# Another instruction order for TensorE, from a planner with other durations, in an attention and gate kernel

## The chip, the core and the metric

The kernel runs on one core of one Trainium2 chip. The metric is the device time of one execution in microseconds. A second figure is the span of the profiled execution, from its first instruction to its last; every time inside the kernel is counted from the start of that span.

## The reference

```python
xn = _layernorm(x, axis=-1)                       # x: 2048 x 640
s = _A_ref(xn, A_wqkv, A_wo)                      # 32 heads of 20
g = _silu(_B_ref(xn, B_w1, B_w2))                 # 640 -> 1536 -> 640
return x + s * g

# _A_ref
scores = jnp.einsum("bhqd,bhkd->bhqk", q, k) * scale
p = _softmax(scores, axis=-1)
o = jnp.einsum("bhqk,bhkd->bhqd", p, v)
# _B_ref
h = jnp.maximum(jnp.einsum("bsd,df->bsf", x, w1), 0)
return jnp.einsum("bsf,fd->bsd", h, w2)
```

x is float32, and so are all weights.

## The kernel before

**Tiling.** The 2048 rows are 16 tiles of 128 rows, taken together as 4 chunks of 512. The 32 heads are 8 groups g of 4 heads, and the 4 heads of a group are two packs of two heads, one on the upper and one on the lower half of the rows of TensorE's array. Products with weights take float32 as two float16 parts, high and low, and add three products (high by high, high by low, low by high).

**Start.** Each tile of x gets its statistics on VectorE (`stats`, L362), a chunk of four tiles its factors (`normal`, L371), and then each tile is scaled on ScalarE, VectorE or POOL (L394, L397). `turn` (L408) transposes a chunk on TensorE (L417); ScalarE writes the high part (the cast of L419), and the low part (xt_lo) is made either by one VectorE operation (L517) or by a ScalarE copy and a POOL subtraction (the "rest" of L522, then L524). Meanwhile the weights of q, k and v get their peaks (`peak_of`, L1075; L229), from which a power of two is made for scaling, with two small products (L244, L256). `piece` (L432) loads 128 columns of a weight and splits them into the two parts: "fast" by ScalarE and VectorE (L280, L282: qh, kh, ql, kl), or else by three POOL operations (L284 to L288). `begin` (L1091) issues this in an order of its own. `first_qk` (L488) makes the first 128 columns of q or k of a chunk (L499); `store` and `load_pack` send them to DRAM and back as packs.

**Middle.** For each group g and chunk c of query rows there are 64 units of scores with their row maxima (L628 on TensorE, a maximum on VectorE, L632). When the 64 are there, the maxima are turned (`rows`, L657; L660) and sent into two more rows of the packed q (the eight transfers of L672, qp<-mhl). Then 64 units of transposed scores follow, from which the maxima are subtracted by those rows (L715 on TensorE, the exponential on ScalarE, L719). Four exponentials are a step; a step is weighed with v by four matmuls in float32 (`weigh`, L743; L751, "pv"). A chunk has 16 steps, the kernel 512, numbered in the names of the tiles pt0 to pt511. After the 16 steps the result is copied out of the accumulator (L763 or L766), turned (L773) and normalised. Between these stands fill: v's products (L329, later L315), the other columns of q and k, the hidden layer of the gate, its output, and the output projection (`out_first`, L998; `out_rest`, L1034), nearly all in the helper `products` (L315), on one half of the array's rows at a time.

**What sets the order.** A planner (`Plan`, L81) runs while the program is written. It holds a clock of its own for TensorE and one for each other engine, the transfers and SyncE; each operation that is written adds its assumed cost (`plan.op`, `plan.pe`, `plan.arrival`). VectorE's small work waits in a list of jobs and is taken by rank, lowest first (`job`, L109). The loop at L1230 looks at what the clocks say is ready: pairs of units (L628, L715) if the engine behind them has less than FULL of work queued, weighing, urgent small turns, the start's generators (`first`), fill (`fill`, rationed by `pace`, L1223). It also lets maxima run at most a set number of units ahead (`mx_start`, L606). The constants at L52 to L78 are the costs: EXP and RED for the exponential and the maximum, BACK for the time until a result is known elsewhere, SWITCH for a change between TensorE's modes. The chip sees only the order: each engine works its list in order and waits on semaphores where data or a buffer is missing.

The lines that the change touches are those constants, the rank of `stats` (L360), the costs at L477 to L480, L595, L874, L958, L960 and L993, and the two pieces at L1110.

Of the kernel before, what the change touches and what calls it, by code (L numbers as in the profile page):

```python
# [17 lines left out]
P = 128  # L18
# [10 lines left out]
TPC = CW // P  # L29
# [21 lines left out]

SWITCH = 100  # L52
LAG = 210
BACK = 90
PAIR = 220
PV = 850
MM = 216
MM_HALF = 136
TURN = 110
EXP = 605  # L60
RED = 640
DMA = 1900
ISSUE = 400
RAGGED = 650
# [93 lines left out]
def attention_gate(ctx: ExitStack, tc: tile.TileContext, x, wqkv, wo, w1, w2, out):  # L158
    nc = tc.nc
    ctx.enter_context(tc.manual_schedule())  # L160
    plan = Plan()
# [194 lines left out]
    def load_x(t, queue="sp"):  # L356
        xs[t] = early.tile([P, D], F32, name=f"x{t}", tag="x", bufs=XS)
        (nc.sync if queue == "sp" else nc.scalar).dma_start(xs[t], x[t * P:(t + 1) * P, :])
        x_landed[t] = plan.arrival(4 * P * D, queue=queue)
        plan.job(30 + 10 * (t // TPC) if t >= TPC else 0, x_landed[t], lambda: stats(t))  # L360

    def stats(t):  # L362
        st = lnp.tile([P, 2, 6], F32, name=f"st{t}", tag="st", bufs=TPC)
# [100 lines left out]
    def qk(m, c):  # L464

        cs = slice(c * CW, (c + 1) * CW)
        sc = SQ / (SX * SW)
        yield from when(lambda: ("q", m) in pieces and ("k", m) in pieces and c in turned)
        ws, at = zip(*(pieces[name, m] for name in "qk"))
        bs, free = take_two()  # L470
        got = yield from products([banks[b] for b in bs], [terms(w, xt, KD, slice(0, P), cs) for w in ws],
                                  max(free, xt_ready[c], *at))
        for name, b in zip("qk", bs):
            hi = stage.tile([P, CW], F16, name=f"hi{name}{m}{c}", tag="hi")
            lo = stage.tile([P, CW], F16, name=f"lo{name}{m}{c}", tag="lo")
            nc.scalar.mul(hi, banks[b], sc)
            done = plan.op("act", 520, got)  # L477
            r = stage.tile([P, CW], F32, name=f"r{name}{m}{c}", tag="r", bufs=2)
            nc.scalar.mul(r, banks[b], sc)  # L479
            bank_free[b] = done = plan.op("act", 520, got)  # L480
            nc.gpsimd.tensor_sub(lo, r, hi)  # L481
            done = plan.op("pool", 1160, done)

            plan.at(done, lambda name=name, hi=hi, lo=lo: store(name, m, c, hi, lo))
# [100 lines left out]
    def v_tiles(n, t):  # L585

        yield from when(lambda: ("v", n) in pieces and t // TPC in turned)
        w, ready = pieces["v", n]
        bs, free = take_two()
        got = yield from products([banks[b][:, 0:HD] for b in bs],  # L590
                                  [terms(xt, w, KD, slice(u * P, (u + 1) * P), slice(0, HD)) for u in (t, t + 1)],
                                  max(free, ready, xt_ready[t // TPC]))
        for u, b in zip((t, t + 1), bs):
            nc.scalar.mul(va[n][:, u, :, 0:DH], banks[b][:, 0:HD].rearrange("p (h d) -> p h d", d=DH), v_scale[n])
            bank_free[b] = v_ready[n, u] = plan.op("act", 450, got)  # L595

# [226 lines left out]
    def gate_hidden():  # L825
# [34 lines left out]
        for f in range(KF):  # L860
            fs = slice(f * P, (f + 1) * P)
            yield from when(lambda: ("1", f) in pieces)
            w, ready = pieces["1", f]
            for pr in range(NC // 2):
                two = [slice(c * CW, (c + 1) * CW) for c in (2 * pr, 2 * pr + 1)]
                bs, free = take_two()
                got = yield from products([banks[b] for b in bs], [terms(w, xt, KD, slice(0, P), cs) for cs in two],
                                          max(free, ready))
                for c, cs, b in zip((2 * pr, 2 * pr + 1), two, bs):
                    r = stage.tile([P, CW], F32, name=f"hr{c}{f}", tag="r", bufs=2)  # L870
                    hi = stage.tile([P, CW], F16, name=f"hh{c}{f}", tag="hi")
                    lo = stage.tile([P, CW], F16, name=f"hl{c}{f}", tag="lo")
                    nc.scalar.activation(r, banks[b], AF.Relu, scale=SH / (SX * SW))  # L873
                    bank_free[b] = done = plan.op("act", 520, got)  # L874
                    nc.gpsimd.tensor_copy(hi, r)  # L875
                    plan.op("pool", 610, done)
                    nc.gpsimd.tensor_sub(lo, r, hi)
                    done = plan.op("pool", 1160)

                    def store(fs=fs, cs=cs, f=f, c=c, hi=hi, lo=lo):  # L880
                        nc.sync.dma_start(h_d["h"][fs, cs], hi)
                        nc.sync.dma_start(h_d["l"][fs, cs], lo)
                        h_stored[f, c] = plan.arrival(2 * 2 * P * CW, 2)

                    plan.at(done, store)
                if pr == 0 and f + 2 < KF:
                    piece("1", w1, f + 2, P)
# [8 lines left out]
    def gate_out():  # L896
# [46 lines left out]
        for c in range(S // HW):  # L943
            ht, ready = nxt
            if c + 1 < S // HW:
                nxt = load_h(c + 1)
            for u in range(HW // P):
                t = c * (HW // P) + u
                gt = gp.tile([P, D], F32, name=f"g{t}", tag="g")
                bs, free = take_two()  # L950
                got = yield from products([banks[b][:, 0:HD] for b in bs],
                                          [terms(ht, w2t, KF, slice(u * P, (u + 1) * P), ns) for ns in halves],
                                          max(free, ready))
                for n, (b, ns) in enumerate(zip(bs, halves)):
                    ps = banks[b][:, 0:HD]
                    th = gp.tile([P, HD], F32, name=f"th{t}{n}", tag="th")
                    nc.scalar.activation(th, ps, AF.Tanh, scale=cz)
                    done = plan.op("act", 540, got)  # L958
                    nc.vector.scalar_tensor_tensor(gt[:, ns], th, 1.0, ps, op0=ALU.add, op1=ALU.mult)
                    bank_free[b] = done = plan.op("dve", 550, done)  # L960

                def store(t=t, gt=gt):
                    nc.sync.dma_start(g_d[t * P:(t + 1) * P, :], gt)
                    g_stored[t] = plan.arrival(4 * P * D)

                plan.at(done, store)
# [13 lines left out]
    def transposed(name, src, ks, ready, tag):  # L980
# [9 lines left out]
            nc.tensor.transpose(pt[:, k, :], src[:, k, :], ident)  # L990
            got = plan.pe("F", TURN, free)
        nc.scalar.mul(oh, pt, SH)
        done = plan.op("act", 520, got)  # L993
        nc.vector.scalar_tensor_tensor(ol, pt, SH, oh, op0=ALU.mult, op1=ALU.subtract)
        bank_free[b] = done = plan.op("dve", 690, done)
        return (oh, ol), done
# [71 lines left out]
    def wide(name):  # L1068
        return wqkv[:, col[name] * D:(col[name] + 1) * D]
# [21 lines left out]
    def begin():  # L1091
# [5 lines left out]
        def next_raw(k):  # L1097
            held.append(raw_load("k", k))
            if k + 1 == KD:
# [7 lines left out]
                    for j in range(2):  # L1107
                        nc.sync.dma_start(kp[i][64 * j + 3 * DH:64 * j + 3 * DH + 2, :], ones_d)
                plan.arrival(9 * 8192, 9)
                for name in "qk":  # L1110
                    piece(name, wide(name), 1, P)

        peak_of("q", 10, [raw_load("q", k) for k in range(KD)], next_raw)
        v_half(0)
# [7 lines left out]
    def settle():  # L1122
# [2 lines left out]
        early_stack.close()  # L1125
        pools["pp"] = pool(ctx, "pp", PTS)
        pools["ep"] = pool(ctx, "ep", 2)
        peaks("1", w1_rows, KF, rawp, 3000, 60000, "wr")
        packs_of(1)
        yield 0  # L1130
# [174 lines left out]
```

## Time and profile before

| | us |
|---|---|
| three runs | 1824.48, 1827.29, 1829.36 |
| median | 1827.29 |
| the profiled execution's own time | 1827.41 |
| its span | 1825.6 |
| TensorE busy | 1756.1 |
| VectorE busy | 1464.2 |
| ScalarE busy | 1397.2 |
| POOL busy | 316.7 |

The engines are PE (TensorE's matmuls), PEld (its weight loads), DVE (VectorE), ACT (ScalarE), POOL and SP (SyncE, which issues nearly all transfers). A row of the timeline gives the start, the length, the engine, the line, the operation, what is written from what, and the count; in brackets stands how long the engine stood idle ahead of it and what released it. Matmuls overlap, so the length of a row is longer than its share of the time: the distance to the next row's start is what counts. Instructions of one kind that follow each other are merged to one row.

### The profile page before, as it was taken

The numbers are of one execution on the slowest core, as the hardware profiler recorded it, in microseconds if no ns is written. First come the engines' busy times: TensorE is split into PE (matmuls) and PEld (weight loads), VectorE is DVE, ScalarE is ACT, GpSimd is POOL, SyncE is SP. The second block draws the span as 40 slices with busy tenths as digits, with TensorE's granted clock in tenths as the row PEclk, the third lists the DMA queues.
The fourth block names the chain that finished last, engine by engine and source line by source line (L and its number), as shares of the span: only waits on it lengthen the run. The fifth ranks groups of instructions, "written<-read, shape, count | busy, mean of one in ns | idle before, by whom it ended". The sixth has DMA issues, their size and how long they took to land.

```text
span 1825.6 us, 37300 instructions
## 1 busy us (share of the span) xinstructions
PE 1756.1 (96%) x14911; PEld 713.9 (39%) x14911; DVE 1464.2 (80%) x2521; ACT 1397.2 (77%) x2328; POOL 316.7 (17%) x339
## 2 busy tenths in 40 slices
PE   5999999999999999999999989999999999999988
PEld 3443334443332433333334234444444443434322
DVE  7598888888887787878887868888888888888961
ACT  2638888788887877888888857877888788786666
POOL 2612200011103454422221130000000000112210
PEclk9999999999999999999999989999999999999999
DMA  7213310201125232311112441211113003224021
GB/s 250 81 58 116 106 48 22 48 20 40 57 64 156 86 106 87 109 35 41 37 35 71 148 112 54 73 33 54 54 47 98 13 19 126 80 80 146 30 71 50
DMA packets 133750, 135.07 MB, mean 74 GB/s; under 512 B 26888, under 2 KB 110232, under 8 KB 133576
## 3 DMA queue, kind: packets, MB, share of 16 engines
q1 hardware_dynamic: 133000, 131.38, 23.6%
q8 instruction: 117, 1.92, 0.4%
q10 hardware_dynamic: 576, 1.31, 0.2%
q14 instruction: 57, 0.47, 0.1%
HBM read 85.07 MB, written 47.33 MB: 73 GB/s over the span
## 4 chain that ended last, share of the span: by engine, by line
PE 87%; ACT 5%; DVE 4%; DMA 3%; issue 1%; POOL 0%; SPq 0%; DVEq 0%; ACTq 0%
PE pv L751 27%; PE ps L315 25%; PE ps L715 15%; PE ps L628 13%; ACT pt L719 4%; PE ps L329 3%; DVE m L632 2%; PE ps L499 2%; DMA hl<-hl_d 1%; PE ps L773 1%; PE ps L990 1%; PE ps L417 0%; DMA 2p<-in_B_w 0%; DMA x<-in_A_x 0%; DMA op<-in_A_wo 0%
## 5 line engine op out<-in xcount | busy, mean ns | idle before, releaser
L632 DVE TENSOR_REDUCE m<-ps 128x1 f32<-128x512 f32 x2048 | 1283.4, 684 | 265.8 <-PE ps L628 259.6
L719 ACT ACTIVATE pt<-ps,cexp 128x512 f32<-128x512 f32 x2048 | 1256.8, 694 | 294.0 <-PE ps L715 204.3
L628 PE MATMUL ps<-kp,qp 60*128 60x512 f16 x2048 | 597.1, 380 | 13.2 <-ACT rest L522 3.9
L715 PE MATMUL ps<-qp,kp 62*128 62x512 f16 x2048 | 588.8, 380 | 5.0 <-ACT pt L719 1.8
L751 PE MATMUL pv<-pt,va 128*21 128x512 f32 x4096 | 542.1, 602 | 0.0
L715 PEld LDWEIGHTS <-kp 62*128 62x128 f16 x2048 | 148.4, 94 | 351.7 <-issue 305.0
L628 PEld LDWEIGHTS <-qp 60*128 60x128 f16 x2048 | 148.2, 94 | 129.0 <-issue 95.3
L751 PEld LDWEIGHTS pv<-pt,va 128*21 128x21 f32 x4096 | 89.6, 99 | 243.7 <-issue 223.3
L315 PE MATMUL ps<-w2th,hl 64*128 64x320 f16 x768 | 123.9, 296 | 2.9 <-DMA hl<-hl_d 2.9
L1027 POOL TENSOR_TENSOR pre<-pre,go 128x320 f32<-128x320 f32 x32 | 26.9, 863 | 572.7 <-DVE go L1025 572.7
L315 PE MATMUL ps<-w2th,hh 64*128 64x320 f16 x768 | 125.8, 296 | 0.3 <-ACT pt L719 0.3
L315 PE MATMUL ps<-w2tl,hh 64*128 64x320 f16 x768 | 124.4, 296 | 0.0
L315 PEld LDWEIGHTS <-hh 64*128 64x128 f16 x1536 | 87.1, 94 | 53.0 <-issue 13.7
L315 PE MATMUL ps<-xt_hi,1h 64*128 64x512 f16 x480 | 103.9, 376 | 0.4 <-ACT pt L719 0.2
L315 PE MATMUL ps<-xt_lo,1h 64*128 64x512 f16 x480 | 101.4, 376 | 0.0
L315 PE MATMUL ps<-xt_hi,1l 64*128 64x512 f16 x480 | 99.7, 376 | 0.0
L875 POOL CAST hh<-hr 128x512 f16<-128x512 f32 x48 | 29.3, 610 | 300.5 <-ACT hr L873 300.5
L315 PEld LDWEIGHTS <-1h 64*128 64x128 f16 x960 | 57.1, 94 | 55.6 <-issue 19.2
L481 POOL TENSOR_TENSOR loq<-rq,hiq 128x512 f16<-128x512 f32 x16 | 18.5, 1157 | 283.5 <-ACT rq L479 283.5
L315 PE MATMUL ps<-xt_hi,kh 64*128 64x512 f16 x150 | 56.4, 376 | 0.1
L315 PE MATMUL ps<-xt_hi,qh 64*128 64x512 f16 x150 | 56.4, 376 | 0.0
L315 PE MATMUL ps<-xt_lo,qh 64*128 64x512 f16 x150 | 56.3, 376 | 0.0
(214 smaller groups left out, 1538.7 us busy)
## 6 DMA issues: line engine op xcount, KB each, us to landing
kp<-k_d SPq DMA_DIRECT2D x28, 240.0 KB
qp<-q_d SPq DMA_DIRECT2D x28, 240.0 KB
hh_d<-hh SPq DMA_DIRECT2D x48, 128.0 KB
hl_d<-hl SPq DMA_DIRECT2D x48, 128.0 KB
hh<-hh_d SPq DMA_DIRECT2D x8, 768.0 KB
hl<-hl_d SPq DMA_DIRECT2D x8, 768.0 KB
q_d<-hiq SPq DMA_DIRECT2D x20, 256.0 KB
k_d<-hik SPq DMA_DIRECT2D x20, 256.0 KB
```

Of the source, the lines that this page charges most:

```text
L315: nc.tensor.matmul(ps[which], a[rows], b[rows], start=(i == 0 and not second), stop=(i == n - 1 and bool(second)))
L329: nc.tensor.matmul(ps[which], a, b, start=(i == 0), stop=(i == len(pairs[which]) - 1))
L481: nc.gpsimd.tensor_sub(lo, r, hi)
L499: nc.tensor.matmul(banks[b], u, v, start=(i == 0), stop=(i == len(pairs) - 1))
L628: nc.tensor.matmul(banks[b], qp[p % RING][r, t:t + P], kp[p % RING][r, kc * CW:(kc + 1) * CW], start=True, stop=True)
L632: nc.vector.tensor_reduce(m4[:, 2 * pr + j, qt, kc:kc + 1], banks[b], axis=AX.X, op=ALU.max)
L715: nc.tensor.matmul(banks[b], kp[p % RING][r, k * P:(k + 1) * P], qp[p % RING][r, c * CW:(c + 1) * CW], start=True, stop=True)
L719: nc.scalar.activation(pt[:, u, :], banks[b], AF.Exp, scale=cexp)
L751: nc.tensor.matmul(pv[32 * h:32 * h + DH + 1, :], va[g // 4][:, k, 4 * (g % 4) + h, :], pt[:, h, :], start=(k == 0), stop=(k == NT - 1))
L773: nc.tensor.transpose(banks[b][:, i * P:(i + 1) * P], sb[:, i * P:(i + 1) * P], ident)
L875: nc.gpsimd.tensor_copy(hi, r)
L1027: nc.gpsimd.tensor_add(pre[:, t, ns], pre[:, t, ns], gts[t][:, ns])
```

## The change

Costs in the plan become other numbers: BACK 90 to 120, EXP 605 to 580, RED 640 to 605, and seven costs of ScalarE and VectorE operations. The statistics of x's second chunk get rank 22 instead of 40 and so go ahead of k's peaks (rank 25); the third and fourth chunk get 40 and 50 instead of 50 and 60. The second pieces of q and k (128 columns each: one load, then three POOL operations) are no longer asked for in `begin`, but in `settle`, when all four chunks are turned. No operation is added or taken away; one tile of x more is scaled by ScalarE and one less by POOL, and six copies of L766 on VectorE become copies of L763 on ScalarE.

```diff
-BACK = 90
+BACK = 120
...
-EXP = 605
-RED = 640
+EXP = 580
+RED = 605
...
-        plan.job(30 + 10 * (t // TPC) if t >= TPC else 0, x_landed[t], lambda: stats(t))
+        plan.job((0, 22, 40, 50)[t // TPC], x_landed[t], lambda: stats(t))
...
-            done = plan.op("act", 520, got)
+            done = plan.op("act", 480, got)
...
-            bank_free[b] = v_ready[n, u] = plan.op("act", 450, got)
+            bank_free[b] = v_ready[n, u] = plan.op("act", 410, got)
...
-                    done = plan.op("act", 540, got)
+                    done = plan.op("act", 420, got)
                     nc.vector.scalar_tensor_tensor(gt[:, ns], th, 1.0, ps, op0=ALU.add, op1=ALU.mult)
-                    bank_free[b] = done = plan.op("dve", 550, done)
+                    bank_free[b] = done = plan.op("dve", 430, done)
...
                 plan.arrival(9 * 8192, 9)
-                for name in "qk":
-                    piece(name, wide(name), 1, P)
...
         pools["ep"] = pool(ctx, "ep", 2)
+        for name in "qk":
+            piece(name, wide(name), 1, P)
         peaks("1", w1_rows, KF, rawp, 3000, 60000, "wr")
```

The first place is VectorE's list at the start, from the low part of q's first piece (ql0) on; kraw0 to kraw4 are the five row blocks of k's weight, x4 to x7 the tiles of the second chunk, st and mv their statistics. Before:

```order
L282 SCALAR_TENSOR_TENSOR ql0_269<-qr0_266,q_inv_261,qh0_268 128x640
L229 TENSOR_REDUCE peakk_265<-kraw1_207 128x1
L229 TENSOR_REDUCE peakk_265<-kraw2_214 128x1
L229 TENSOR_REDUCE peakk_265<-kraw3_217 128x1
L229 TENSOR_REDUCE peakk_265<-kraw4_263 128x1
L239 TENSOR_REDUCE k_pk_347<-peakk_265 128x1
L365 BN_STATS st4_357<-x4_168 128x6 x2
L366 BN_AGGR mv1_138<-st4_357 128x2
L248 TENSOR_REDUCE k_top_348<-ps5_71 1x1
```

And the same place now:

```order
L282 SCALAR_TENSOR_TENSOR ql0_269<-qr0_266,q_inv_261,qh0_268 128x640
L365 BN_STATS st5_325<-x5_170 128x6 x2
L366 BN_AGGR mv1_138<-st5_325 128x2
L365 BN_STATS st6_336<-x6_172 128x6 x2
L366 BN_AGGR mv1_138<-st6_336 128x2
L365 BN_STATS st7_345<-x7_174 128x6 x2
L366 BN_AGGR mv1_138<-st7_345 128x2
L375 TENSOR_SCALAR v1_349<-mv1_138 128x4
L229 TENSOR_REDUCE peakk_265<-kraw0_199 128x1
L381 RECIPROCAL r1_350<-r1_350 128x4
```

The second chunk's statistics moved from behind k's peaks to ahead of them (those of x4 stand a few rows further up), and k's scale comes out later. On ScalarE the high part of k's first piece (kh0) moves with it, from behind q's first result to behind the second chunk's five casts and rests. On TensorE k's first product (L499 on kh0) moves from ahead of that chunk's turns to behind them.

The second place is the end of TensorE's list, where the maxima of the last chunk of the last group are turned (L660); pt494 and the like are steps, pvs and on the results of a chunk, oh and ol parts of the output projection's operand, ot a tile of it. Before:

```order
L715 LDWEIGHTS kp3_106
L715 MATMUL ps2_68<-qp3_110,kp3_106 128x512
L751 MATMUL pv_65<-pt494_19986,va1_142 21x512 x4
L660 MATMUL ps0_66<-ident_73,m_73_20007 16x128
L751 MATMUL pv_65<-pt495_20009,va1_142 21x512 x4
L773 MATMUL ps5_71<-ident_73,pvs72_20038 128x128 x4
L990 MATMUL ps4_70<-ident_73,on72_20040 128x128 x4
L329 LDWEIGHTS ohr2_20057
L329 MATMUL ps3_69<-wo_h_11436,ohr2_20057 128x320
```

And now:

```order
L715 LDWEIGHTS kp3_106
L715 MATMUL ps1_67<-qp3_110,kp3_106 128x512
L773 MATMUL ps0_66<-ident_73,pvs71_19447 128x128 x4
L660 MATMUL ps4_70<-ident_73,m_73_19455 16x128
L315 LDWEIGHTS ol10_19198
L315 MATMUL ps2_68<-wo_h_11542,ol10_19198 128x320
L315 LDWEIGHTS ol10_19198
L315 MATMUL ps5_71<-wo_h_11542,ol10_19198 128x320
L990 MATMUL ps3_69<-ident_73,ot12_19192 128x128 x4
L751 MATMUL pv_65<-pt482_19457,va1_142 21x512 x4
```

The turn of the last maxima moved from behind step 494 to behind step 481, with output projection of tile 10 still to come where before all of it was done.

More of the change, by code (lines that the diff above doesn't have):

```diff
@@ L476, in qk @@
             nc.scalar.mul(hi, banks[b], sc)
-            done = plan.op("act", 520, got)
+            done = plan.op("act", 480, got)
             r = stage.tile([P, CW], F32, name=f"r{name}{m}{c}", tag="r", bufs=2)
             nc.scalar.mul(r, banks[b], sc)
-            bank_free[b] = done = plan.op("act", 520, got)
+            bank_free[b] = done = plan.op("act", 480, got)
             nc.gpsimd.tensor_sub(lo, r, hi)
@@ L873, in gate_hidden @@
                     nc.scalar.activation(r, banks[b], AF.Relu, scale=SH / (SX * SW))
-                    bank_free[b] = done = plan.op("act", 520, got)
+                    bank_free[b] = done = plan.op("act", 480, got)
                     nc.gpsimd.tensor_copy(hi, r)
@@ L992, in transposed @@
         nc.scalar.mul(oh, pt, SH)
-        done = plan.op("act", 520, got)
+        done = plan.op("act", 480, got)
         nc.vector.scalar_tensor_tensor(ol, pt, SH, oh, op0=ALU.mult, op1=ALU.subtract)
```

## The prediction

> **What bounds the kernel now.** I read the page's head first, then the windows of the span, then the timelines of TensorE, ScalarE, VectorE and SyncE where a window is loose, and the list of waits last. The windows' columns are stretch and length, then busy time (count) of PE, PEld, DVE, ACT and POOL, the granted clock, and the DMA's share and GB/s.
>
> ```profile
> span 1825.6 us, 37300 instructions
> PE 1756.1 (96%) x14911; PEld 713.9 (39%) x14911; DVE 1464.2 (80%) x2521; ACT 1397.2 (77%) x2328; POOL 316.7 (17%) x339
> ```
> ```profile
> 569.70:573.10 3.40, 3.40 (x17) 0.67 (x13) 1.71 (x3) 1.73 (x3) 0.00 (x0) 0.50 0.51 169
> 47.80:62.00 14.20, 10.34 (x39) 4.16 (x40) 10.73 (x33) 9.67 (x19) 8.53 (x8) 0.76 0.09 26
> 127.90:1592.90 1465.00, 1442.17 (x12741) 585.61 (x12738) 1213.62 (x2053) 1186.04 (x1971) 229.58 (x240) 0.99 0.23 68
> 1592.90:1715.40 122.50, 119.38 (x1084) 50.26 (x1085) 104.31 (x183) 85.39 (x141) 28.39 (x35) 1.00 0.32 102
> 1715.40:1758.90 43.50, 41.94 (x282) 11.03 (x276) 38.12 (x65) 38.65 (x64) 3.95 (x5) 1.00 0.04 15
> 1758.90:1770.70 11.80, 6.17 (x24) 2.50 (x23) 3.78 (x7) 0.60 (x1) 1.46 (x2) 0.73 0.37 120
> 1770.70:1809.40 38.70, 38.14 (x203) 8.97 (x202) 2.39 (x6) 37.20 (x64) 5.18 (x7) 0.99 0.21 72
> ```
>
> TensorE bounds the middle: 1442 of 1465 us, ScalarE 1186. The end is different. From 1592.9 to 1715.4 TensorE is full while ScalarE has 85 of 122 us; then the roles turn: 1715.4 to 1758.9 ScalarE has 64 exponentials in 38.65 us, 11.8 us hold one ScalarE instruction, and the last 64 exponentials fill 37.2 of 38.7 us. A busy TensorE row there overstates it, as the counts of matmuls (203 in 38.7 us, against 1084 in 122.5) show.
>
> So I price TensorE by instructions. These rows (start, length, operation, count) give the prices:
>
> ```profile
> 557.75 0.39 PE L715 MATMUL ps<-qp,kp 62*128 62x512 f16 x2
> 558.07 1.92 PE L751 MATMUL pv<-pt,va 128*21 128x512 f32 x16
> 559.92 0.39 PE L715 MATMUL ps<-qp,kp 62*128 62x512 f16 x1
> ...
> 564.30 0.38 PE L315 MATMUL ps<-xt_hi,1h 64*128 64x512 f16 x2
> 564.52 0.40 PE L715 MATMUL ps<-qp,kp 62*128 62x512 f16 x2
> 564.85 1.06 PE L751 MATMUL pv<-pt,va 128*21 128x512 f32 x8
> 565.84 0.39 PE L715 MATMUL ps<-qp,kp 62*128 62x512 f16 x1
> 568.86 0.37 PE L628 MATMUL ps<-kp,qp 60*128 60x512 f16 x1 [2.63 <-DVE m L632]
> ...
> 1062.03 0.30 PE L315 MATMUL ps<-w2tl,hh 64*128 64x320 f16 x2
> 1062.17 0.30 PE L315 MATMUL ps<-w2th,hl 64*128 64x320 f16 x2
> ```
>
> A pair on half the rows each, 512 columns, takes 0.22 us (564.30 to 564.52), one of 320 columns 0.14. A block of weighing (L751) costs 0.11 more ahead of it (0.33 to 564.85), 0.99 for one step and 1.85 for two (558.07 to 559.92): 0.86 a step and 0.13 a block, so 0.24, taken as 0.23, for each block beyond the steps. A turn (L417, L773, L990) is 0.12, by the row of 12 at 62.06 below (1.47); a run of turns changes the mode like a block, 0.2. A matmul of L329 counts as a pair of 320 columns.
>
> **The change part by part: the middle and the costs of the planner.** The plan's costs are not waits; they only set the order. Counted in TensorE's order, L751 stands in 405 blocks before and 371 now. I cut the order at every 64th L715, the 64 exponentials of one group and chunk, and call each part a stage. In stages 1 to 28 (127.9 to 1592.9) stood 1790 pairs of L628 and L715, 1170 pairs of 512 and 1524 of 320 columns of L315, 448 steps in 344 blocks, and 176 turns in 72 runs; by the prices above some 1357 us of 1465. Now stand there 1826, 1170, 1468, 447 in 314, and 164 in 70: +36 pairs (+7.9), -56 (-7.6), -1 step (-0.9), -30 blocks (-6.9), -12 turns and -2 runs (-1.8), so **-9**. The other 108 us are waits and frictions, of which these are the longest:
>
> ```profile
> PE ps L244 <- DVE o_pk L239: 4.2, 1, 4.2
> PE ps L628 <- DVE m L632: 3.7, 5, 2.6
> PE ps L315 <- DMA hl<-hl_d: 2.9, 1, 2.9
> PE ps L628 <- ACT pt L719: 2.2, 10, 0.3
> ...
> PE ps L715 <- DVE m L632: 1.7, 5, 0.8
> ```
>
> The same loads stand before the same peaks and products now, and I take these waits as unchanged. From below: were they gone with the half clock that follows such a wait (the window at 569.7 shows 0.50 for 3.4 us, a loss of 1.7), the middle would give some 12 more. From above, as much again would take all of the 9 back.
>
> **The end.** The second pair of rows of TensorE's order in the section on the change shows it: the last maxima are turned (L660) behind step 494 before, behind step 481 now. When the last L628 has run, 68 L715 and no L315 are left before; now 120 and 198. All through the middle the maxima run further ahead: when those of one chunk are complete, 8 to 30 exponentials are still missing of the chunk ahead of it before, in most chunks 40 to 90 now. Before, the end runs like this:
>
> ```profile
> 1758.22 4.97 SPq L672 DMA_DIRECT2D qp<-mhl  x8
> ```
> ```profile
> 1752.64 2.48 DVE L632 TENSOR_REDUCE m<-ps 128x1 f32<-128x512 f32 x4 [0.23 <-PE ps L628]
> ```
> ```profile
> 1770.75 1.26 ACT L719 ACTIVATE pt<-ps,cexp 128x512 f32<-128x512 f32 x2 [3.46 <-PE ps L715]
> 1773.41 35.94 ACT L719 ACTIVATE pt<-ps,cexp 128x512 f32<-128x512 f32 x62 [1.40 <-PE ps L715]
> ```
>
> The row maxima of the last chunk go to memory tile qp by eight transfers from 1758.2; the exponentials that need them start at 1770.75, and nothing else is left for either engine. Stages 29 and 30 took 122.5 us, 31 and 32 to the last exponential 94.0 (1715.4 to 1809.4), in all 216.5.
>
> By count, in stages 29 and 30 before: 126 pairs (27.7), 237 of 320 and 48 of L329 (38.5 at 0.135), 32 steps (27.5), 31 blocks (7.1), 54 turns in 25 runs (11.5): 112 us of TensorE, 10 less than measured. In 31 and 32 up to the last L715: 92, 15 + 24, 30 in 29, 9 in 2: 59 us, where ScalarE alone has 128 x 0.58 = 74 (62 exponentials in 35.94). Now: 114, 172 + 24, 32 in 26, 41 in 19: 94 us, and 69, 112 + 72, 31 in 30, 33 in 11: 80. So the same work is spread: 174 us of TensorE over four stages in which ScalarE has 39 each. With the 9% that the TensorE-bound half runs over its count that is 189; the last seven steps hold exponentials alone, 4 x 0.58 against 1.5 of TensorE, where some 5 us of ScalarE stay bare. 216.5 - 194 = **-22**. Bounds: -28 with ScalarE fully hidden and little friction, -10 if both engines, now nearly equal there, hinder each other on every step. The 16 us behind the last exponential keep their order.
>
> **The start.** Before, TensorE waits for banks while ScalarE drains chunk 1's turns, and goes on at half clock:
>
> ```profile
> 35.59 0.30 PE L329 MATMUL ps<-vh,xt_hi 128*128 128x320 f16 x1
> ...
> 47.80 2.41 PE L417 MATMUL ps<-ident,x 128*128 128x128 f32 x18 [0.15 <-POOL x L397]
> 53.00 0.37 PE L628 MATMUL ps<-kp,qp 60*128 60x512 f16 x1 [2.79 <-ACT rest L522]
> 54.44 0.58 PE L628 MATMUL ps<-kp,qp 60*128 60x512 f16 x1 [1.06 <-ACT rest L522]
> ...
> 62.06 1.47 PE L417 MATMUL ps<-ident,x 128*128 128x128 f32 x12
> ```
> ```profile
> 38.47 0.83 ACT L280 ACTIVATE kh<-kr,k_inv 128x640 f16<-128x640 f32 x1 [1.59 <-DVE k_inv L264]
> 48.90 0.58 ACT L419 CAST xt_hi<-ps 128x512 f16<-128x512 f32 x1
> 53.79 0.60 ACT L522 ACTIVATE rest<-ps 128x512 f32<-128x512 f32 x1 [0.36 <-POOL xt_lo L524]
> ```
> ```profile
> 39.33 1.02 DVE L282 SCALAR_TENSOR_TENSOR kl<-kr,k_inv,kh 128x640 f16<-128x640 f32 x1 [0.25 <-DMA q_d<-hiq]
> 40.27 0.87 DVE L365 BATCH_NORM_STATS2 st<-x 128x6 f32<-128x320 f32 x2
> 41.30 0.83 DVE L365 BATCH_NORM_STATS2 st<-x 128x6 f32<-128x320 f32 x2
> ```
>
> Between 47.80 and 62.06 stand 18 turns (2.2), 15 products of L499 (3.2) and three pairs with two mode changes each (1.3): 6.7 of 14.3 us, a loss of 7.6. Now chunk 1's statistics (1.03 us a tile, 40.27 to 41.30) run ahead of k's peaks, so its tiles are scaled near 39.5 (ql near 30.7, three tiles of statistics, k's first peak and six small operations to 36; then q's casts and three scalings on ScalarE), while TensorE still has 36 products of v behind q's (35.6 + 0.3 for the tile that now delays v's peak + 4.9 = 40.8). The turns then stand without a wait, with v products after them. What is late next is k's first piece: in ScalarE's order kh now stands behind all five casts and rests, which took 48.90 to 54.39, 5.5 us. They begin at 41.4, kh ends at 47.7, kl at 48.7. TensorE needs kh at 46.5 (20 turns, 18 products of v, two of q behind 40.8): it waits 1.2 and then about 1 for kl. Behind kl on VectorE stand chunk 2's statistics, which are needed 6 us later. The half clock on top costs 0 to 3.4 us: 1.7 taken. -7.6 + 0.3 + 2.2 + 1.7 = -3.4, say **-4** with the half microsecond of waits ahead of 47.80; from -6 to +1.
>
> The trace has half clock after 2.63 us of waiting (568.86, then the window at 0.50). The Trainium skill, TensorE: Matmul & The Clock Gate, section "HAM oscillation", sets the limit at idle gaps of about 3.4 us. By that rule two waits of 1 us would cost no clock, and the start would give 5 to 6; this trace shows a shorter wait doing it, and it decides.
>
> The second pieces of q and k (two loads, six POOL instructions) move behind chunk 3's turns. On POOL the last lows of k and q queue behind them, on SyncE the stores of q's third chunk. I cost that at nothing: chunk 3 of k is wanted by the 49th L628; by my sum those run at 1.2 us a pair on VectorE from some 72 on, so at 100, and the splits end near 85; the pieces themselves are wanted behind v's products, past 115. If that cover were gone, VectorE would wait up to 3 us, with v's products still there for TensorE.
>
> **Sum.** 1825.6 - 4 - 9 - 22 = 1790.6 of span; the profiled run took 1827.41, 1.8 more than its span, and lies 0.1 over the median of 1827.29. Forecast: **1792**.
>
> **The rivals.** *No slack left, slower.* The plan had 605 and 640 ns for the exponential and the maximum where the rows give 580 (35.94 for 62) and 600 (2.48 for 4); with 580 and 605 TensorE is sent to a bank just when it should be free, and any late instruction stops it in front of queued fill. At 0.095 us for each of 371 blocks the gain of 35 is gone; at 0.13 the time is 1840. Against it: the three rows of waits for L632 and L719 above add up to 7.6 us, 0.02 a block, and the assumed delay until a bank is free grows by 30 ns. *The end's fill is itself late*, its loads queued on SyncE behind stores that wait for POOL: no gain at the end, 1814. For it: all of out_first's loads share that one queue; against it: they stand several tiles ahead. *The middle's waits go as well*, since VectorE no longer runs ahead of the plan into loads not landed: 1780. *It does nothing*: frictions take the middle's 9, and the end gives under 10: 1818 to 1827.
>
> **How the numbers follow.** Forecast 0.68, the fill late 0.13, middle's waits gone 0.08, nothing 0.05, no slack 0.06. The forecast's own terms reach from -6 - 21 - 28 (1772) to +1 + 0 - 10 (1818), seldom all at once; 1775 to 1815 takes in the second and third rival and leaves out the last two. About 0.3% (5.5 us) is what a measurement can tell from no change: faster 0.89, same 0.05, slower 0.06.
>
> **What would show it.** Right: no wait of 2.8 us for L522 near 50, instead waits of about 1 for kh and kl near 47; the first exponential near 124; stages 29 to 32 within 200 us to the last exponential; no stretch of 10 us without exponentials behind the last maximum. Wrong: TensorE's waits for L632 and L719 in the middle above 30 us, or the last 64 exponentials spread over more than 50 us with TensorE waiting for transfers.

## The result, and the profile after

The changed kernel takes 1794.23 us (median of four runs, 1793.59 to 1795.73), the kernel before, on the same chip, 1827.72 (four runs, 1824.48 to 1829.36). The ratio is 0.982 with an interval of 0.9803 to 0.9837; the forecast was 1792.

The head of the page after, and the windows of the span after, cut at the same events as before: stages 1 to 28, 29 and 30, 31, 32, and the stretch at the start (columns as in the prediction):

```profile
span 1792.5 us, 37247 instructions
PE 1737.7 (97%) x14887; PEld 725.2 (40%) x14887; DVE 1453.0 (81%) x2515; ACT 1391.3 (78%) x2335; POOL 315.7 (18%) x338
```
```profile
122.80:1579.30 1456.50, 1440.13 (x12679) 597.57 (x12680) 1241.24 (x2111) 1179.01 (x1975) 226.67 (x236) 1.00 0.23 67
1579.30:1682.00 102.70, 101.33 (x897) 41.21 (x893) 81.50 (x140) 81.99 (x138) 18.80 (x23) 1.00 0.31 100
1682.00:1729.10 47.10, 46.45 (x405) 17.40 (x399) 18.50 (x35) 40.18 (x69) 11.73 (x14) 1.00 0.34 117
1729.10:1776.10 47.00, 46.47 (x331) 15.17 (x330) 9.61 (x19) 40.52 (x69) 11.68 (x14) 1.00 0.17 59
47.00:62.00 15.00, 13.80 (x79) 7.99 (x80) 10.79 (x32) 10.51 (x20) 7.72 (x7) 1.00 0.25 76
```

The first exponential's product comes at 122.8 instead of 127.9: 5.1 gained. Stages 1 to 28 take 1456.5 instead of 1465.0: 8.5. Stages 29 to 32 to the last exponential take 196.8 instead of 216.5: 19.7. The rest behind it is 16.4 instead of 16.2. The sum is 33.1, and the span fell by 33.1. TensorE now has 736 matmuls in stages 31 and 32 (405 and 331) where it had 509; VectorE, 38.1 us busy from 1715.4 to 1758.9 before, mostly with maxima, is busy for 18.5 in stage 31 with other work. The granted clock, 0.76 in the start's stretch before, is 1.00. The work of TensorE is the same, but not its form: 48 products on half the array (L315) are now 24 on the whole of it (L329), so there are 24 matmuls fewer; by the prediction's price, one of L329 as a pair, they cost the same.

The timelines of TensorE and ScalarE at the start after:

```profile
47.24 0.39 PE L499 MATMUL ps<-xt_hi,kh 128*128 128x512 f16 x1 [0.80 <-ACT kh L280]
47.47 0.38 PE L499 MATMUL ps<-xt_lo,kh 128*128 128x512 f16 x1
48.81 0.39 PE L499 MATMUL ps<-xt_hi,kl 128*128 128x512 f16 x1 [0.96 <-DVE kl L282]
...
46.37 0.82 ACT L280 ACTIVATE kh<-kr,k_inv 128x640 f16<-128x640 f32 x1
```

The 2.79 and 1.06 us for L522 are gone; k's first piece is what is late, by 0.80 and 0.96 us, and no half clock follows. The timelines of SyncE and ScalarE at the end after:

```profile
1695.23 4.90 SPq L672 DMA_DIRECT2D qp<-mhl  x8
...
1736.13 2.57 ACT L719 ACTIVATE pt<-ps,cexp 128x512 f32<-128x512 f32 x4
1741.87 0.60 ACT L992 ACTIVATE oh<-ps 128x512 f16<-128x512 f32 x1 [3.17 <-PE ps L990]
1743.96 8.20 ACT L719 ACTIVATE pt<-ps,cexp 128x512 f32<-128x512 f32 x14 [1.49 <-PE ps L715]
```

The last maxima leave at 1695.2, 34 us before the exponentials that need them (stage 32, from 1729). The hole of 11.8 us is gone; the longest stretch without exponentials there is 5.3 us (1738.7 to 1744.0). The list of waits after has these rows in place of the five of before:

```profile
PE ps L715 <- DVE m L632: 6.4, 4, 3.1
PE ps L715 <- ACT pt L719: 2.6, 12, 0.6
...
PE ps L628 <- ACT pt L719: 2.5, 10, 0.7
...
PE ps L628 <- DVE m L632: 1.3, 1, 1.3
...
PE ps L315 <- DMA hl<-hl_d: 0.3, 1, 0.3
```

### The profile page after: what moved, and what is told of

It is laid out like the page before. It is cut to its first block, busy times and chain, and to the rows that moved or that the text cites. A ratio compares the mean times of both kernels' runs of the same rounds, so it can differ in the third digit from the quotient of the medians.

```text
span 1792.5 us, 37247 instructions
## 1 busy us (share of the span) xinstructions
PE 1737.7 (97%) x14887; PEld 725.2 (40%) x14887; DVE 1453.0 (81%) x2515; ACT 1391.3 (78%) x2335; POOL 315.7 (18%) x338
## 4 chain that ended last, share of the span: by engine, by line
PE 88%; ACT 5%; DVE 3%; DMA 2%; SPq 1%; issue 1%; POOL 0%; DVEq 0%; ACTq 0%
PE pv L751 26%; PE ps L315 26%; PE ps L715 16%; PE ps L628 13%; ACT pt L719 4%; PE ps L329 3%; PE ps L499 1%; PE ps L773 1%; SPq L209 1%; DVE m L632 1%; DMA op<-in_A_wo 1%; PE ps L990 1%; DMA 2p<-in_B_w 1%; DVE st L365 0%; DMA x<-in_A_x 0%
## 5 line engine op out<-in xcount | busy, mean ns | idle before, releaser
L719 ACT ACTIVATE pt<-ps,cexp 128x512 f32<-128x512 f32 x2048 | 1250.8, 689 | 300.8 <-PE ps L715 258.9
L632 DVE TENSOR_REDUCE m<-ps 128x1 f32<-128x512 f32 x2048 | 1274.8, 683 | 215.7 <-PE ps L628 206.8
L628 PE MATMUL ps<-kp,qp 60*128 60x512 f16 x2048 | 591.3, 378 | 5.8 <-ACT pt L719 2.5
L715 PE MATMUL ps<-qp,kp 62*128 62x512 f16 x2048 | 582.8, 380 | 9.8 <-DVE m L632 6.4
L751 PE MATMUL pv<-pt,va 128*21 128x512 f32 x4096 | 522.5, 599 | 0.0
L715 PEld LDWEIGHTS <-kp 62*128 62x128 f16 x2048 | 148.3, 93 | 332.2 <-issue 292.8
L628 PEld LDWEIGHTS <-qp 60*128 60x128 f16 x2048 | 151.3, 94 | 114.4 <-issue 78.4
L751 PEld LDWEIGHTS pv<-pt,va 128*21 128x21 f32 x4096 | 89.6, 100 | 236.9 <-issue 223.0
L315 PE MATMUL ps<-w2th,hl 64*128 64x320 f16 x768 | 128.8, 295 | 0.3 <-DMA hl<-hl_d 0.3
L315 PE MATMUL ps<-w2th,hh 64*128 64x320 f16 x768 | 128.6, 295 | 0.1
L315 PE MATMUL ps<-w2tl,hh 64*128 64x320 f16 x768 | 128.2, 295 | 0.0
L315 PEld LDWEIGHTS <-hh 64*128 64x128 f16 x1536 | 90.8, 94 | 53.2 <-issue 13.2
L315 PE MATMUL ps<-xt_hi,1h 64*128 64x512 f16 x480 | 104.1, 378 | 0.1
L315 PE MATMUL ps<-xt_lo,1h 64*128 64x512 f16 x480 | 102.8, 377 | 0.0
L315 PE MATMUL ps<-xt_hi,1l 64*128 64x512 f16 x480 | 100.1, 376 | 0.0
L315 PEld LDWEIGHTS <-1h 64*128 64x128 f16 x960 | 57.5, 94 | 57.4 <-issue 22.3
L315 PE MATMUL ps<-xt_hi,kh 64*128 64x512 f16 x150 | 56.3, 376 | 0.3
L315 PE MATMUL ps<-xt_lo,qh 64*128 64x512 f16 x150 | 56.3, 376 | 0.0
L315 PE MATMUL ps<-xt_hi,qh 64*128 64x512 f16 x150 | 56.3, 376 | 0.0
```

The source lines that it names most:

```text
L315: nc.tensor.matmul(ps[which], a[rows], b[rows], start=(i == 0 and not second), stop=(i == n - 1 and bool(second)))
L628: nc.tensor.matmul(banks[b], qp[p % RING][r, t:t + P], kp[p % RING][r, kc * CW:(kc + 1) * CW], start=True, stop=True)
L632: nc.vector.tensor_reduce(m4[:, 2 * pr + j, qt, kc:kc + 1], banks[b], axis=AX.X, op=ALU.max)
L715: nc.tensor.matmul(banks[b], kp[p % RING][r, k * P:(k + 1) * P], qp[p % RING][r, c * CW:(c + 1) * CW], start=True, stop=True)
L719: nc.scalar.activation(pt[:, u, :], banks[b], AF.Exp, scale=cexp)
L751: nc.tensor.matmul(pv[32 * h:32 * h + DH + 1, :], va[g // 4][:, k, 4 * (g % 4) + h, :], pt[:, h, :], start=(k == 0), stop=(k == NT - 1))
```

## The experiments

The table holds what the twelve runs turn on. "Count" is TensorE's work by the prediction's method over the whole program, with prices fitted a little finer to the trace of before (0.226 us for a pair of L628 or L715, 0.22 and 0.137 for pairs of L315, 0.857 a step, 0.1 for each change of mode). A product of L329 with 512 columns, which starts 0.22 us after the one before it, stands there at the price of 320 columns; so the counts of experiments 7 and 8, with 30 more of these, and that of stages 1 to 28 in experiment 2, with 22 more, are some 2 us low. "Over" is the span of the profiled run less the count, and "over, 1-28" the same for stages 1 to 28. "Left" is the number of L715 behind the last L628, a measure of the lead at the end. Ratios are against the kernel before on the same chip, with their intervals.

| kernel | L751 blocks | count | over | over, 1-28 | left | stages 29-32 | median us | ratio |
|---|---|---|---|---|---|---|---|---|
| before | 405 | 1623.9 | 201.7 | 102 | 68 | 216.4 | 1827.7 | |
| after | 371 | 1615.7 | 176.8 | 103 | 120 | 196.7 | 1794.2 | 0.982 (0.9803 to 0.9837) |
| 1 start only | 400 | 1622.0 | 201.5 | 100 | 68 | 209.4 | 1821.1 | 0.9967 (0.9954 to 0.9979) |
| 2 costs only | 374 | 1616.5 | 179.6 | 107 | 116 | 192.3 | 1797.3 | 0.9841 (0.9825 to 0.9856) |
| 3 EXP new, RED old | 377 | 1617.2 | 221.2 | 117 | 68 | 215.8 | 1839.9 | 1.0078 (1.0062 to 1.0095) |
| 4 RED new, EXP old | 404 | 1622.6 | 176.1 | 99 | 104 | 197.7 | 1800.2 | 0.9853 (0.984 to 0.9867) |
| 5 555 and 575 | 363 | 1614.5 | 182.4 | 116 | 142 | 191.7 | 1796.6 | 0.9847 (0.9832 to 0.9861) |
| 6 lead capped | 376 | 1617.1 | 190.0 | 105 | 66 | 217.2 | 1808.7 | 0.9913 (0.9899 to 0.9928) |
| 7 longer queues | 336 | 1603.2 | 245.0 | 172 | 150 | 187.9 | 1850.2 | 1.0139 (1.0122 to 1.0156) |
| 8 and late peaks | 334 | 1603.4 | 241.3 | 168 | 150 | 187.9 | 1846.3 | 1.0115 (1.01 to 1.013) |
| 9 BACK 90 | 399 | 1620.5 | 162.2 | 95 | 102 | 203.8 | 1785.4 | 0.9773 (0.9759 to 0.9788) |
| 10 FULL 1100 | 367 | 1615.7 | 179.7 | 106 | 84 | 204.1 | 1795.5 | 0.9829 (0.9814 to 0.9844) |
| 11 STOCK 1300 | 321 | 1602.9 | 233.6 | 154 | 136 | 191.3 | 1840.4 | 1.0075 (1.0059 to 1.0092) |
| 12 BACK 120 alone | 409 | 1624.5 | 190.0 | 91 | 66 | 210.1 | 1820.3 | 0.996 (0.9946 to 0.9973) |

**1 and 2, the start and the costs apart.** Experiment 1 is the kernel before with

```diff
-        plan.job(30 + 10 * (t // TPC) if t >= TPC else 0, x_landed[t], lambda: stats(t))
+        plan.job((0, 22, 40, 50)[t // TPC], x_landed[t], lambda: stats(t))
...
-                for name in "qk":
-                    piece(name, wide(name), 1, P)
...
+        for name in "qk":
+            piece(name, wide(name), 1, P)
         peaks("1", w1_rows, KF, rawp, 3000, 60000, "wr")
```

> The kernel before with the two edits at the start (rank of the second chunk's statistics, second pieces of q and k asked for later) and the old costs of the plan. TensorE's order then has 400 blocks of L751 (before 405, after 371), and behind the last L628 stand 68 L715 and no L315, as before: the maxima don't run ahead. Theory of the parts (start, middle and end come from different edits): the first exponential comes near 123.5 as in the kernel after (128.3 before), and the maxima's lead at the end stays short, with a hole of about 10 us without exponentials behind the last maximum. By the prices of the prediction the middle's count is 12 us more than before and the end's 15 less, since the changed start also reshuffles what follows, so 1815 to 1823 in all. Rival: the edits at the start are what brings most of the gain, the planner's costs only shift work about: under 1805.

Experiment 2 is the changed kernel with these lines as before, all costs new.

> The changed kernel with the start as before (old rank, pieces in their old place) and all of the new costs. 374 blocks of L751; behind the last L628 stand 116 L715 and 220 L315. Theory of the parts: the 2.8 us wait for L522 near 50 is back or a like one, first exponential at 125 to 128; the end (stages 29 to 32) again takes 194 to 198 us instead of 216, no hole; 1798 to 1803 in all. Rival (the start is what pays): over 1812.

Measured: 1821.1 and 1797.3. The start alone gives 6 us, the costs alone 30, both 33.5. In experiment 1 the first exponential's product is at 122.8, the middle is 1474.9 us, 10 more than before, where its count (1374.9 against 1362.9) said 12, and the end 7 less. (Its profiled run is the slowest of its six, 4 us over their median, and the table's "over" holds these 4 us.) In experiment 2 the start's waits stand as before, and its window from 54 has the half clock:

```profile
52.70 0.37 PE L628 MATMUL ps<-kp,qp 60*128 60x512 f16 x1 [2.80 <-ACT rest L522]
54.06 0.58 PE L628 MATMUL ps<-kp,qp 60*128 60x512 f16 x1 [0.99 <-ACT rest L522]
```
```profile
54.00:58.00 4.00, 3.94 (x9) 0.81 (x9) 3.44 (x11) 1.72 (x4) 2.48 (x3) 0.50 0.00 0
```

Yet its first exponential's product comes at 122.9 too, since some 4 us less of TensorE's work stands ahead of it (22 fewer products of L329 with 512 columns, at 0.22). That mark, on which the prediction set its test of the start, is moved by the order as well as by the waits; the waits themselves and the clock are the safe test.

**3 and 4, the two big costs apart.** Each is the changed kernel with one constant as before:

```diff
-RED = 605
+RED = 640
```

> The changed kernel with the maximum's cost back at 640, the exponential's at its new 580. 377 blocks of L751, nearly as few as after (371), but behind the last L628 stand only 68 L715 and no L315, as before. Theory (the maxima's lead fills the end): the end has its hole of about 10 us again, stages 29 to 32 take 203 to 210 us, the middle's count is 13 us above that of after; 1810 to 1820 in all. Rival (what pays is that TensorE changes its mode less often): 6 blocks at 0.23 us more than after, so 1794 to 1798.

```diff
-EXP = 580
+EXP = 605
```

> The changed kernel with the exponential's cost back at 605, the maximum's at its new 605. 404 blocks of L751, as many as before (405), but behind the last L628 stand 104 L715 and 162 L315. Theory (the maxima's lead fills the end): stages 29 to 32 take 196 to 201 us without a hole, the middle's count is 9 us above that of after; 1800 to 1808 in all. Rival (fewer mode changes pay, the lead does not): the 33 blocks more than after cost 8 and the end its 20, so 1818 to 1824.

Measured: 1839.9, which neither side had, and 1800.2, as the theory had it. The rival of "fewer mode changes" fails on both: 377 blocks with the old RED are 46 us slower than after and 12 slower than before, and 404 blocks with the new RED are 6 slower than after. The lead comes from RED: with a maximum assumed at 640 the plan puts maxima off, and their lead is 7 to 20 units through the second half and 0 to 4 at the end. The end of experiment 3, SyncE and ScalarE, reads as before's did:

```profile
1770.25 4.97 SPq L672 DMA_DIRECT2D qp<-mhl  x8
...
1767.35 3.58 ACT L719 ACTIVATE pt<-ps,cexp 128x512 f32<-128x512 f32 x6 [0.29 <-PE ps L628]
1778.72 0.60 ACT L992 ACTIVATE ohr<-ps 128x512 f16<-128x512 f32 x1 [7.80 <-PE ps L990]
1782.78 1.26 ACT L719 ACTIVATE pt<-ps,cexp 128x512 f32<-128x512 f32 x2 [3.46 <-PE ps L715]
```

From 1770.9 to 1782.8 ScalarE has one instruction. That explains its end (215.8). That its middle runs 117 over the count, 14 more than after, was not expected, and my figure of 1810 to 1820 missed by 20; it lies in stage 1 (9.7 us over the count, 5.2 in after), stage 9 (11.2 and 6.6) and stages 24 to 27 (16.5 and 8.4), the others being about as in after. Why is open.

**5, lower still.** The changed kernel with

```diff
-EXP = 580
-RED = 605
+EXP = 555
+RED = 575
```

> The changed kernel with the plan's costs lower still, below what the rows show: 555 for the exponential, 575 for the maximum. 363 blocks of L751 (after 371), maxima up to 100 exponentials ahead, 142 L715 and 216 L315 behind the last L628. In the runs so far the span is TensorE's count plus 176 to 180 us in every kernel with a lead at the end. Theory (count and lead decide): count 1614.5 against 1615.7, so the time of after less 1, 1790 to 1796. Rival (no slack left in the plan: TensorE is sent to banks that are not free): 0.05 us or more for each of 363 blocks, 1812 or more, with waits for L632 and L719 above 30 us in the middle.

Measured: 1796.6, its interval overlapping that of after. The count's 1 us and 5 us of the end (191.7) are eaten by 13 us more over the count in stages 1 to 28. So some of the rival's friction is there, 0.036 us for each of 363 blocks, not the 0.05 and more that would have decided.

**6, the lead capped.** The changed kernel with

```diff
-LEAD = 80
+LEAD = 40
```

> The changed kernel with LEAD 40 in place of 80, which caps how far the maxima may run ahead; all costs as in after. 376 blocks of L751 and a count of TensorE's work of 1617.1 us against 1615.7, but the maxima are complete only 18 to 25 exponentials ahead through the middle and 0 to 4 at the end; 66 L715 and 24 L315 stand behind the last L628. Theory (the lead fills the end): stages 29 to 32 take 215 to 225 us with the hole of about 10 us back, the middle (more fill left for the end) is 6 to 8 us shorter than that of after; 1806 to 1816 in all. Rival (the lead at the end is beside the point, fewer mode changes and costs that agree with the chip pay): 1.4 us more than after, 1794 to 1797.

Measured: 1808.7, as the theory had it. All costs are those of after, the count differs by 1.4, and the end takes 217.2 instead of 196.7; the middle is 6 shorter (1450.5), because more fill is left for stages 29 to 31. In the windows of its stages 31 and 32 TensorE's work lies in the first:

```profile
1696.70:1752.80 56.10, 53.82 (x490) 23.81 (x489) 45.44 (x80) 41.02 (x68) 14.75 (x19) 1.00 0.20 66
1752.80:1790.40 37.60, 37.35 (x191) 7.93 (x190) 1.03 (x3) 37.09 (x64) 4.56 (x6) 1.00 0.21 73
```

ScalarE's last 64 exponentials fill 37 us in which TensorE runs 191 matmuls, where after has 405 and 331 in the two stages. This is the end's mechanism by itself: a cap on the lead, and nothing else, costs 20 us there and 14 in all.

**7, 8, 10 and 11, longer and shorter queues.** Since each block saved is worth 0.2 us in the count, I tried to save more of them. Experiment 7 is the changed kernel with the first two edits, 8 has the other two beside.

```diff
-FULL = 1300
+FULL = 1700
-STOCK = 900
+STOCK = 1200
...
-        peaks("2", lambda k: w2[k * P:(k + 1) * P, :], KF, late, 2500)
+        peaks("2", lambda k: w2[k * P:(k + 1) * P, :], KF, late, 5000, 6000)
...
-        peaks("o", lambda k: wo[k * P:(k + 1) * P, :], KD, gp, 3000)
+        peaks("o", lambda k: wo[k * P:(k + 1) * P, :], KD, gp, 6000, 8000)
```

> The changed kernel with FULL 1700 in place of 1300 and STOCK 1200 in place of 900: ScalarE and VectorE get longer queues before TensorE turns to weighing, so more steps are weighed at a time. 336 blocks of L751 (after 371), the maxima about 100 exponentials ahead from stage 8 on. TensorE's count is 1603.2 us against 1615.7. Theory (count plus 177): 12 us less than after, 1779 to 1785. Rival (longer queues hold the banks, and TensorE waits for them): no gain or a loss, 1794 or more, with waits for L632 and L719 that after does not have.

> The kernel with longer queues (FULL 1700, STOCK 1200), and beside it the loads of the peaks of w2 and wo start later (6 and 8 us) and stand further apart (5 and 6 us instead of 2.5 and 3), so that VectorE does not stand at a peak whose load has not landed while maxima queue behind it. Count 1603.4 us. In after stage 9 runs 6.6 us and stage 18 runs 15.3 us over the count, the other stages 3 us. Theory: stage 9 falls to about 4 and stage 18 to about 9 over the count, 6 to 10 us less than the kernel with longer queues alone. Rival: what holds stage 18 is the lack of fill until wo's and the hidden layer's loads have landed, so TensorE stands elsewhere instead: same time within 3 us.

Experiments 10 and 11 part the two constants, each the changed kernel with one of them:

```diff
-FULL = 1300
+FULL = 1100
```

> The changed kernel with FULL 1100 instead of 1300: shorter queues for ScalarE and VectorE. 367 blocks of L751, the same count as after (1615.7), a lead of 50 to 60 in the second half, 84 L715 and 114 L315 behind the last L628. Theory (waits for banks that the list of waits does not show grow with the length of the queues): stages 1 to 17 run 50 to 58 us over the count instead of 63 in after and 120 in the kernel with longer queues; 1784 to 1791. Rival (at 1300 no bank is missed, and the longer-queues kernel lost by weighing later): 1793 to 1797.

```diff
-STOCK = 900
+STOCK = 1300
```

> The changed kernel with STOCK 1300 instead of 900 and FULL as in after: weighing starts only when both engines have 1.3 us of work queued, so more steps are weighed at a time; 321 blocks of L751, count 1602.9 us against 1615.7, 136 L715 and 102 L315 behind the last L628. Theory (it was FULL 1700 that made TensorE run into banks not yet free): the count's 13 us come through, 1780 to 1786. Rival (weighing late is what costs, since TensorE must first fill the queues to the brim and meets banks that are not free): stages 1 to 17 run 90 to 120 us over the count, 1815 to 1845.

Measured: 1850.2, 1846.3, 1795.5 and 1840.4. Experiments 7, 8 and 11 have the best counts and a good end and are, with experiment 3, the slowest: stages 1 to 17 run 120, 119 and 105 us over the count, against 63 after. With FULL untouched and STOCK alone raised the loss is there, and with FULL lowered nothing is gained (64), so late weighing costs by itself. What FULL 1700 adds in experiment 7 was not tried alone. Experiment 8 is 4 us below 7, and takes 2 from stage 18 where I expected 6, and nothing from stage 9: moving the peaks' loads is not what that stage wants. That it wants fill, as the rival has it, was not tried alone.

The timelines of TensorE, ScalarE and VectorE in experiment 11 show one place where it loses:

```profile
302.45 0.38 PE L715 MATMUL ps<-qp,kp 62*128 62x512 f16 x1
302.65 0.37 PE L628 MATMUL ps<-kp,qp 60*128 60x512 f16 x1
302.92 0.37 PE L715 MATMUL ps<-qp,kp 62*128 62x512 f16 x1
303.27 0.37 PE L628 MATMUL ps<-kp,qp 60*128 60x512 f16 x1
303.52 0.37 PE L715 MATMUL ps<-qp,kp 62*128 62x512 f16 x1
303.85 0.37 PE L628 MATMUL ps<-kp,qp 60*128 60x512 f16 x1
...
300.76 4.82 ACT L719 ACTIVATE pt<-ps,cexp 128x512 f32<-128x512 f32 x8 [1.66 <-PE ps L715]
...
300.98 5.47 DVE L632 TENSOR_REDUCE m<-ps 128x1 f32<-128x512 f32 x9 [1.09 <-PE ps L628]
```

From 302.45 to 303.85 TensorE starts six units, 0.28 apart, where a unit costs 0.11: two in 0.5 to 0.6 us, which is ScalarE's and VectorE's own pace (4.82 for 8, 5.47 for 9, both without a pause). It has filled their queues and now follows them instead of weighing. No row carries a wait in brackets: the modelled lengths of 0.37 cover the gaps. This place is not the whole of it. Priced from start to start over stages 1 to 17, experiment 11 loses some 30 us more than after between fill and the next unit, and 11 more in the units just ahead of weighing; only 7 of the 30 stand at units that start within 0.08 us of the release they waited for. That the two engines' pace holds TensorE in all these places is therefore argued and not shown. Nor does experiment 11's list of waits show it:

```profile
PE ps L628 <- DVE m L632: 5.0, 3, 3.7
PE ps L628 <- ACT pt L719: 4.0, 18, 0.4
PE ps L715 <- ACT pt L719: 2.3, 10, 0.3
PE ps L715 <- DVE m L632: 0.4, 1, 0.4
```

These make 11.7 us; the middle runs 154 over its count. The windows call TensorE 99% busy there:

```profile
122.10:1052.50 930.40, 923.50 (x7319) 354.72 (x7320) 767.00 (x1306) 724.02 (x1229) 204.19 (x211) 1.00 0.21 64
```

The Trainium skill, Perfetto Trace Analysis, section "Identifying the Most-Contended Engine", warns that the busy share of matmuls is not a good measure of how close a kernel is to its roofline, because they are pipelined. This trace agrees, with 923.5 of 930.4 us busy and 105 of them over the count.

**9 and 12, BACK.** Experiment 9 is the changed kernel, experiment 12 the kernel before, each with the other's value:

```diff
-BACK = 120
+BACK = 90
```

> The changed kernel with BACK, the assumed delay until a result is known elsewhere, at its old 90 instead of 120. 399 blocks of L751, a lead of 40 to 60 exponentials in the second half and 102 L715 and 144 L315 behind the last L628. Count of TensorE's work 1620.5 us against 1615.7. Theory (count and lead): 5 us more than after, 1796 to 1803. Rival (BACK keeps TensorE from running into results that are not there yet): its waits in the middle grow by 10 us or more on top, 1808 or more.

```diff
-BACK = 90
+BACK = 120
```

> The kernel before with BACK 120 instead of 90 and nothing else. 409 blocks of L751 (before 405), count of TensorE's work 1624.5 us (before 1623.9), lead and end as in before: 66 L715 and no L315 behind the last L628. With the other new costs, 120 instead of 90 cost 9 us against a count that is 5 less: 14 us of time beyond the count. Theory (the longer assumed delay makes TensorE pass by banks that are free on the chip, whatever the other costs): 8 to 16 us slower than before, 1834 to 1842. Rival (it was one stretch, such as the loads of wo's peaks, that fell badly in the order with 120 and the new costs): 1823 to 1831.

Measured: 1785.4 and 1820.3 (the profiled run of 12, with a span of 1814.5, is at the quick end of its runs). Both expectations failed. The changed kernel without its BACK is 9 us faster than with it, the fastest of all (the two intervals don't meet), though its count is 5 us higher; yet the same BACK alone makes the kernel before 8 us faster. So BACK 120 has no price of its own. Experiment 9's list of waits has no row for o_pk, hl or L715 behind a maximum above 0.4 us, and its middle, with a good lead, runs 95 over the count:

```profile
121.20:1557.30 1436.10, 1423.16 (x12465) 582.50 (x12464) 1221.54 (x2067) 1178.69 (x1975) 227.60 (x236) 1.00 0.22 64
1557.30:1761.10 203.80, 200.42 (x1666) 80.13 (x1662) 124.16 (x221) 166.49 (x280) 41.83 (x50) 1.00 0.34 114
```

The 14.6 us beyond the count are spread: 4 in stages 1 to 17, 4 in the rest of the middle, 3 at the end, 3 behind the last exponential, 1 at the start. I can't name one cause.

## Why the prediction was right, step by step

**The start: right, a little small.** Forecast -4, measured -5.1. The turns stand at 40.66 (forecast 40.8), kh ends at 47.2 (47.7), the waits are 0.80 and 0.96 (1.2 and 1). The 1.7 us for half clock did not fall due: the clock is 1.00 in the window. That fits the rule of the Trainium skill, TensorE: Matmul & The Clock Gate, section "HAM oscillation", and the start's 5 to 6 by it; but its limit of 3.4 us of idling is still not what the traces show, since in experiment 2 a wait of 2.80 us and one of 0.99 are again followed by a window at 0.50. Nor does the length of a wait decide it alone: after's 3.14 us at 562.44 is followed by 0.50 from 563.75 to 567.15, its 2.53 us at 1063.82 by 1.00, and from 1034.8 to 1038.2 it has 0.50 behind no listed wait above 0.4. Experiment 1 shows that the two edits bring this gain without the costs.

**The second pieces at nothing: not contradicted.** They were not tried alone; the list of waits after has no row of TensorE behind the splits on POOL, and none behind a transfer above 0.3 us.

**The middle: the size right, the premise wrong.** Forecast -9, measured -8.5. I took the long waits as unchanged. They were not: the 4.2 us for o_pk are gone, the 2.9 for hl are 0.3, and stage 18 as a whole takes 55.9 us instead of 61.5 while its count rose by 1.7, so 7 us fell away. The other 27 stages gave the same back: 88 us over their count where it was 80. Part of it is L715's wait for a maximum (6.4 us, 1.7 before); its two longest, 3.14 at 562 and 2.53 at 1064, stand where VectorE is held by peaks whose loads are late, as the waits of the kernel before did under other names (TensorE, then VectorE):

```profile
562.44 0.37 PE L715 MATMUL ps<-qp,kp 62*128 62x512 f16 x1 [3.14 <-DVE m L632]
...
1063.82 0.37 PE L715 MATMUL ps<-qp,kp 62*128 62x512 f16 x1 [2.53 <-DVE m L632]
...
560.97 0.82 DVE L229 TENSOR_REDUCE peak<-2p 128x1 f32<-128x640 f32 x1 [2.43 <-DMA 2p<-in_B_w]
...
1062.35 0.82 DVE L229 TENSOR_REDUCE peako<-op 128x1 f32<-128x640 f32 x1 [2.32 <-DMA op<-in_A_wo]
```

What gave back the rest is open. So two errors of 7 and 8 us cancelled; that the sum came within 0.5 us of the forecast is luck, and the rival "the middle's waits go as well" was half true.

**The blocks: the price right, their role too large.** Experiment 4 against after prices it: the same time over the count, 33 blocks and 6.2 us apart, 0.19 a block. But experiments 3, 7 and 11 have few blocks and are slower than before.

**The end: right, and the main term.** Forecast -22 (194 us), measured -19.7 (196.8). Stages 29 and 30 take 102.7 us, 9% over the 94 of the prediction's count, as it assumed; stages 31 and 32 take 94.1 where 80 with the 9% and the 5 bare us gave 92. By the table's count for stages 29 to 32 alone, every kernel in the table with 66 or 68 L715 left runs 35 to 55 us over it there, every one with 84 or more 20 to 32. Experiments 3 and 6 take the lead away by two different constants and lose the end both times. The rival "the end's fill is itself late" did not come: the list of waits after has no row behind a transfer above 0.3 us.

**The rival "no slack left": not here, but real.** Its price was to decide from 0.095 us a block. After pays 0.02 (8 us over 371 blocks outside stage 18). One figure under it was misread: 2.48 us for 4 maxima are 620 ns each and not 600 (experiment 11 has 5.47 for 9, 608 each), so the new 605 lies just below the rows and leaves less slack than I thought. In experiments 7 and 11 the same kind of thing costs some 70 and 52 us more than in before, 0.2 and 0.16 a block: there the forecast would have been turned round. The sign that I set for it, waits for L632 and L719 above 30 us, would have missed it; those rows come to 12 us in experiment 11.

## What to carry to other kernels

Where a plan sets an in-order engine's list, look first at whether the program's last stretch still has work for it, and at which constant decides how early the feeding work runs: here a maximum assumed at 640 ns instead of 605 kept the maxima back and left some 20 us at the end bare. Price a new order by counts stage by stage, and measure what lies over the count, for a list of waits and a busy share can both look clean while some 50 us are lost in gaps of 0.1 to 0.3 us between matmuls. Constants of one plan don't add up, so take each back from the whole as well as trying it alone: one that gained 8 us by itself cost 9 in company.

## What the runs showed that I had not expected

The split that makes kl on VectorE took 1.02 us in before and took 1.53 after, while POOL was busy with the five subtractions of L524:

```profile
47.22 1.53 DVE L282 SCALAR_TENSOR_TENSOR kl<-kr,k_inv,kh 128x640 f16<-128x640 f32 x1 [2.29 <-ACT kh L280]
...
42.46 5.61 POOL L524 TENSOR_TENSOR xt_lo<-rest,xt_hi 128x512 f16<-128x512 f32 x5 [3.31 <-ACT rest L522]
```

Experiments 1 and 9 show 1.53 in the same place, experiment 2, where kl stands as in before, 1.02. The Trainium skill, SBUF — State Buffer, section "SBUF: two separate sides", says that a VectorE operation with two inputs in SBUF and a POOL operation that reads SBUF lock each other out for a whole instruction; half a microsecond more fits that. So does ql, an operation of the same shape, which took 0.88 us at 28.99 after, where POOL stood idle (14.3 to 37.1). In before POOL was at work beside kl too, with a cast and a subtraction, and that subtraction (39.75, L288) took 1.85 us where the like one for k took 1.40. No run here took POOL's work away from kl itself.
